# A second-layer feed-forward kernel: split weights kept in DRAM, background work put between a maximum and its split, the last two pairs' operands used in place

## The chip, the cores and the metric

The kernel runs on one core of a Trainium2 chip. The metric is the device time of one execution in microseconds (us). A profile is one further execution, recorded by the hardware profiler; its span runs from its first to its last instruction. Engines are TensorE (PE), VectorE (DVE), ScalarE (ACT), GpSimd (POOL) and SyncE (SP, which here only issues DMAs).

## What is computed

The reference is a gated linear attention (4 batches, 8 heads, 768 steps, head width 48), then a mixture of 8 experts, one for each token, and then a dense feed-forward layer, the "second layer", which is what the change is about:

```python
def _moe2_ref(x, w_in, w_out):      # x: 3072 x 384, w_in: 384 x 2048, w_out: 2048 x 384
    h = x @ w_in
    g = np.maximum(0.01 * h, h)
    return (g @ w_out).astype(np.float32)
```

## The kernel before, in words

All products are float32 in three passes: an operand is split into a rounded high part (`hi`, cast on ScalarE) and a remainder (`lo`, a subtraction on VectorE or GpSimd), and hi·hi, hi·lo and lo·hi are accumulated. That is the helper `split` (L145 the cast, L146 the subtraction).

The program has three stages: the attention (to about 200 us), the experts (to about 381 us) and the second layer, `ffn` (from 381 us to the end). Every engine runs its instructions in the order of the program; SP too issues its DMAs in that order, each after its own waits.

The 3072 tokens of the second layer are cut into six tiles of 512 (`NJ`), the 2048 hidden units into 16 blocks of 128 (`FB`).

**Plain tiles 0 and 1.** The loop counts blocks, n = 0 to 31, 16 for each tile. Block n: nine 512-column products into one of two PSUM banks by turns (L1075); ScalarE makes 0.01·h (`t`, L1079); VectorE takes the maximum of `t` and the bank (L1080), which frees the bank for block n+2; `split` makes `g` of it; the next block's `w_out` rows are split into a tile `wos` (`wosplit`, cast on ScalarE, subtraction on GpSimd); then the second product of block n-2, twelve 384-column products (L1144) into four accumulators (`oacc`); then `more(2)`, two steps of background work. When a tile's last block is done, VectorE and ScalarE copy the accumulators out (L1151); two of the four banks of tile 1's accumulators are banks that tile 0's have used.

**The background** is a generator of steps, mostly on VectorE: first the decoding of the 64-bit weights (L743 to L766, four steps for each half-block), of which 24 steps are left when `ffn` begins; then eight times `forms(m)`: sums and differences of the blocks of pair m's `w_in` (`sums`, L775 to L784) that are split (`forms`: cast L785, subtraction L787) and stored to DRAM (`wfd`). `sums` and `forms` share two buffers (`xw`).

**Tiles 2 to 5** take blocks in pairs, q = 16 to 47, with fewer products: each pair combines its `forms`, loaded back from DRAM into `wf` (L1061), with sums of the tile's columns (`bsum`, `bform`; `bstep` makes those of the next tile). A pair is 33 products of 256 columns (L1088) and 24 of 384 columns (L1144), and splits two blocks' `w_out` rows with `wosplit`. The `wf` of a pair is loaded into one of two `xw` buffers after the last product of the pair two before. The first two, for q = 16 and 17, are loaded at n = 29 and n = 31, after the last `forms`.

Of the kernel before, what the change touches and what calls it, by code (L numbers as in the profile page):

```python
# [83 lines left out]
def kernel(  # L84
# [627 lines left out]
    def experts_and_ffn(place):  # L712
        with ExitStack() as st:
# [5 lines left out]
            wi = [wb.tile([128, 2, 768], FP32R, name=f"wi{i}") for i in range(NM)]  # L719
            wo = [wb.tile([128, 384], FP32, name=f"wo{i}") for i in range(FB)]  # L720
            y = yb.tile([128, 3, NT + GW], FP32, name="y")
# [8 lines left out]
            def decode(i):  # L730
# [34 lines left out]
                if i >= FB:  # L765
                    nc.vector.tensor_tensor(out=wo[i - FB], in0=af, in1=b, op=ALU.add)  # L766
                yield

            def forms(m):

                w = wi[m]
                r = mw.tile([128, 9, 128], FP32, tag="xw", name="sums", bufs=2)
                f = mw.tile([128, 5, 2, 128], FP32R, tag="xw", name="forms", bufs=2)
                tt = nc.vector.tensor_tensor
                tt(out=r[:, 5:9, :].rearrange("p a c -> p (a c)"), in0=w[:, 0, 128:640].bitcast(FP32),  # L775
                   in1=w[:, 1, 128:640].bitcast(FP32), op=ALU.add)
                yield
                a0, b0, a1, b1 = (r[:, 5 + i, :] for i in range(4))
                rr = r[:, 5:9, :].rearrange("p (h i) c -> p h i c", h=2)
                tt(out=r[:, 0:2, :], in0=rr[:, :, 0, :], in1=rr[:, :, 1, :], op=ALU.add)  # L780
                tt(out=r[:, 2, :], in0=a0, in1=b1, op=ALU.add)
# [250 lines left out]
            def bform(j, f):  # L1032
# [3 lines left out]
                else:  # L1036
                    two = ((4, 5), (0, 1), (2, 3), (6, 7), (8, 8))
                    k = [f in x for x in two].index(True)
                    if (j, k) not in bfs:
                        bfs[j, k] = mw.tile([128, 2, 2, HW], FP32R, tag="xT", name="bf", bufs=6)  # L1040
                    t = bfs[j, k][:, two[k].index(f)]
                split(t[:, 0, :], t[:, 1, :], src, nc.vector)
                bfs[j, "f", f] = t

            BSTEPS = {1: ((0, 1), (4,)), 2: ((2, 3), (5,)), 3: ((8,), (0,)), 4: ((), (1, 6)), 5: ((), (2, 7)),
                      6: ((), (3,)), 7: ((), (8,))}

            def bstep(j, m, k):
                for f in BSTEPS.get(m, ((), ()))[k]:
                    (bform if k else bsum)(j, f)  # L1050

            M, NQ = NJ * FB, NJ * NM

            def ffn(key, rest, plain):
                gT, oacc, wos, wf, cap = {}, {}, {}, {}, {}
                tt = nc.vector.tensor_tensor

                def wload2(q):
                    if q < NQ:
                        wf[q] = mw.tile([128, 5, 2, 128], FP32R, tag="xw", name="wf", bufs=2)  # L1060
                        nc.sync.dma_start(out=wf[q].bitcast(FP32), in_=wfd[q % NM])  # L1061

                def wosplit(n):
                    if n < M:
                        w = mw.tile([128, 2, 384], FP32R, tag=f"w{n % 2}", name="wos")
                        split(w[:, 0, :], w[:, 1, :], wo[n % FB], nc.gpsimd)
                        wos[n] = w

                def f1(n):
# [10 lines left out]
                    tt(out=t, in0=t, in1=h_ps, op=ALU.max)  # L1080
                    split(g[:, 0, :], g[:, 1, :], t, nc.vector)
                    gT[n] = [g[:, :, s * 128:(s + 1) * 128] for s in range(4)]

                def mul(q, reg, a, b, first=False):
                    w, x = wi[q % NM], bfs[q // NM, "f", b]
                    c = {5: 128, 6: 512, 7: 0, 8: 640}.get(a)
# [100 lines left out]
                if not plain:  # L1187
                    for m in BSTEPS:
                        for k in range(2):
                            bstep(0, m, k)  # L1190
                    wload2(0)
                    wload2(1)
                for q in range(plain * NM, NQ):
                    j, m = divmod(q, NM)
                    start(q)
                    if q == plain * NM:
                        wosplit(2 * q + 1)
                    wosplit(2 * q + 2)
# [105 lines left out]
```

## Time and profile before

| | |
|---|---|
| median of 3 runs | 795.43 us (795.07 to 795.74) |
| the profiled execution | 797.1 us, of which the span is 795.3 us |
| busy, share of the span | PE 765.3 us (96%), DVE 630.0 (79%), ACT 413.7 (52%), POOL 229.0 (29%) |
| DMA | 112.46 MB, 141 GB/s over the span |
| chain that ended last | PE 70%, DVE 17%, issue 6%, ACT 5%, DMA 1%, POOL 1% |

The profiled execution took 1.7 us more than the median run, and 1.8 us of its time lie outside the span. In a row of the trace the first number is the start in us from the span's start, the second the time from start to end; `x9` are nine instructions merged; `[2.50 <-DVE y L1151]` is idle time of the engine just before, and what ended it. The busy share says little here: TensorE is near its full share in every stage, so the question is in which stretch it stands still.

### The profile page before, as it was taken

Reading aid. Unit: us, or ns where it says so; the run is one execution under the profiler, and the core shown is the slowest. Engines: PE = TensorE matmul, PEld = TensorE weight load, DVE = VectorE, ACT = ScalarE, POOL = GpSimd, SP = SyncE. Lnnn points to the kernel's source line nnn. Section 1 sums busy time; section 2 is a strip of 40 time slices with the busy share of each in tenths; the row PEclk is TensorE's granted clock in tenths of the full one; section 3 lists DMA queues with packets and bytes.
Section 4 is the critical chain, followed back from the end, with each engine's and each line's share of the span. In section 5 each row is a group of like instructions: output and inputs, shape, how many; then the busy total and the mean of one; then the engine's idle time right before and its main releaser. Section 6 shows DMA issues by size and latency. Waiting matters only on the chain.

```text
span 795.3 us, 15530 instructions
## 1 busy us (share of the span) xinstructions
PE 765.3 (96%) x5694; PEld 723.6 (91%) x5695; DVE 630.0 (79%) x1269; ACT 413.7 (52%) x944; POOL 229.0 (29%) x241
## 2 busy tenths in 40 slices
PE   6999998999999999999999999979999999999996
PEld 6888886899999999999889887779999999999996
DVE  8999997668889899989688777768769768766664
ACT  6688775565665656555343344453535444444432
POOL 1322286341111112121222242243233315223221
PEclk9799999999999999999999999999999999999999
DMA  9998834466678678865020021142223233324221
GB/s 347 303 304 281 312 122 130 147 204 212 122 206 212 154 185 216 200 180 140 21 59 21 34 106 66 67 153 90 97 77 129 67 100 106 101 67 132 74 68 44
DMA packets 43221, 112.46 MB, mean 141 GB/s; under 512 B 8256, under 2 KB 19328, under 8 KB 43136
## 3 DMA queue, kind: packets, MB, share of 16 engines
q1 hardware_dynamic: 39296, 101.93, 42.5%
q0 software_dynamic: 3840, 9.47, 3.2%
q8 instruction: 46, 0.75, 0.4%
q14 instruction: 39, 0.32, 0.2%
HBM read 90.36 MB, written 21.01 MB: 140 GB/s over the span
## 4 chain that ended last, share of the span: by engine, by line
PE 70%; DVE 17%; issue 6%; ACT 5%; DMA 1%; POOL 1%; DVEq 0%; POOLq 0%; ACTq 0%; SPq 0%
PE oacc L1144 17%; PE r L1088 15%; PE acc L346 12%; PE h L331 12%; PE A L465 3%; PE X L529 3%; PE Y L519 2%; DVE t L1080 2%; PE Y L513 2%; ACT g L145 2%; DVE g L146 2%; DVE d_t L763 1%; DVE kh L442 1%; DVE sums L775 1%; PE h L1075 1%
## 5 line engine op out<-in xcount | busy, mean ns | idle before, releaser
L1144 PE MATMUL oacc<-wos,g 128*128 128x384 f32 x1152 | 223.1, 338 | 2.5 <-DVE y L1151 2.5
L1144 PEld LDWEIGHTS oacc<-wos,g 128*128 128x128 f32 x1152 | 198.9, 188 | 5.6 <-DVE y L1151 2.8
L146 POOL TENSOR_TENSOR wos<-wo,wos 128x384 fp32r<-128x384 f32 x96 | 100.2, 1059 | 257.8 <-ACT wos L145 254.0
L346 PE MATMUL acc<-hT,w 128*128 128x224 f32 (+7 forms) x648 | 122.5, 333 | 1.4 <-DVE hT L335 1.4
L331 PE MATMUL h<-xT,w 128*128 128x224 f32 (+7 forms) x576 | 114.4, 342 | 0.4 <-DVE w L279 0.4
L346 PEld LDWEIGHTS acc<-hT,w 128*128 128x128 f32 x648 | 109.1, 189 | 4.8 <-DVE hT L335 2.3
L331 PEld LDWEIGHTS h<-xT,w 128*128 128x128 f32 x576 | 98.8, 189 | 3.3 <-DVE w L279 1.0
L273 ACT CAST w<-wraw 128x384 fp32r<-128x384 f32 x138 | 67.5, 513 | 23.4 <-PE acc L346 20.0
L279 DVE TENSOR_TENSOR w<-wraw,w 128x384 fp32r<-128x384 f32 x138 | 72.0, 560 | 6.1 <-ACT w L273 5.2
L1075 PE MATMUL h<-ysp,wi 128*128 128x512 f32 x288 | 72.7, 398 | 3.7 <-DVE t L1080 3.7
L1088 PE MATMUL r<-bf,wi 128*128 128x256 f32 x480 | 68.9, 279 | 0.0
L1075 PEld LDWEIGHTS h<-ysp,wi 128*128 128x128 f32 x288 | 53.1, 188 | 16.1 <-DVE t L1080 5.6
L1123 ACT COPY c<-r 128x256 f32<-128x256 f32 x32 | 11.9, 372 | 107.2 <-PE r L1088 107.2
L1088 PEld LDWEIGHTS r<-bf,wi 128*128 128x128 f32 x480 | 62.6, 188 | 0.0
L334 ACT ACTIVATE hT<-h 128x224 fp32r<-128x224 f32 (+7 forms) x64 | 31.6, 493 | 39.6 <-PE h L331 37.9
L145 ACT CAST g<-t 128x512 fp32r<-128x512 f32 x32 | 19.9, 621 | 62.1 <-DVE t L1080 62.1
L965 POOL COPY seen<-hT 1x1 f32<-1x1 f32 x26 | 7.4, 283 | 150.6 <-DVE hT L335 150.6
L1126 DVE SCALAR_TENSOR_TENSOR c<-c 128x512 f32<-128x512 f32 x64 | 41.4, 688 | 9.8 <-ACT c L1123 8.9
L145 ACT CAST g<-c 128x512 fp32r<-128x512 f32 x64 | 39.2, 622 | 15.4 <-DVE c L1126 14.9
L335 DVE SCALAR_TENSOR_TENSOR hT<-h,hT 128x224 fp32r<-128x224 f32 (+7 forms) x64 | 35.7, 557 | 14.1 <-ACT hT L334 14.1
L449 POOL TENSOR_TENSOR kh<-fkq,kh 128x512 f32<-128x512 f32 x22 | 26.3, 1194 | 70.6 <-DVE kh L442 52.3
L145 ACT CAST wos<-wo 128x384 fp32r<-128x384 f32 x96 | 46.1, 515 | 0.0
(172 smaller groups left out, 1336.7 us busy)
## 6 DMA issues: line engine op xcount, KB each, us to landing
wraw<-in_wpk SPq DMA_DIRECT2D x69, 384.0 KB
wf<-wfd SPq DMA_DIRECT2D x32, 640.0 KB
fkq<-in_fkq SPq DMA_DIRECT2D x21, 770.5 KB
xs<-zero SPq DMA_DIRECT2D x16, 385.0 KB
raw<-in_w_in SPq DMA_DIRECT2D x16, 384.0 KB
raw<-in_w_out SPq DMA_DIRECT2D x16, 384.0 KB
wfd<-forms SPq DMA_DIRECT2D x8, 640.0 KB
v<-in_v SPq DMA_DIRECT2D x24, 192.0 KB
```

The lines of the kernel that those rows point to most:

```text
L145: nc.scalar.copy(out=hi, in_=src)
L146: eng.tensor_tensor(out=lo, in0=src, in1=hi.bitcast(FP32), op=ALU.subtract)
L273: nc.scalar.copy(out=w[:, 0, :], in_=wraw[n][:, 384 * i:384 * (i + 1)])
L279: nc.vector.tensor_tensor(out=w[:, 1, :], in0=r[:, 384 * i:384 * (i + 1)], in1=w[:, 0, :].bitcast(FP32), op=ALU.subtract)
L331: nc.tensor.matmul(out=h_ps, lhsT=w[:, a, kk * 128:(kk + 1) * 128], rhs=xT[p][kk][:, b, :], start=(kk == 0 and a + b == 0), stop=(kk == 2 ...
L334: nc.scalar.activation(out=t[:, 0, :], in_=h_ps, func=ACTF.Relu)
L335: nc.vector.scalar_tensor_tensor(out=t[:, 1, :], in0=h_ps, scalar=0.0, in1=t[:, 0, :].bitcast(FP32), op0=ALU.max, op1=ALU.subtract)
L346: nc.tensor.matmul(out=a_ps[d], lhsT=w[:, a, d * 128:(d + 1) * 128], rhs=t[:, b, :], start=(j == 0 and a + b == 0), stop=(j == KF - 1 and ...
L1075: nc.tensor.matmul(out=h_ps, lhsT=wi[i // 2][:, a, c:c + 128], rhs=ysp[j][kk][:, b, :], start=(kk == 0 and a + b == 0), stop=(kk == 2 and ...
L1088: nc.tensor.matmul(out=reg, lhsT=wf[q][:, a, s, :] if c is None else w[:, s, c:c + 128], rhs=x[:, t, :], start=first and k == 0, stop=k == ...
L1126: nc.vector.scalar_tensor_tensor(out=c, in0=c, scalar=0.01, in1=c, op0=ALU.mult, op1=ALU.max)
L1144: nc.tensor.matmul(out=oacc[j][s], lhsT=gT[n][s][:, b, :], rhs=wos[n][:, a, :], start=i == 0 and a + b == 0, stop=i == FB - 1 and (a, b) = ...
```

## The change

1. `wosplit` splits a block's `w_out` rows only in tile 0, and stores both halves to a DRAM tensor `wod`. From tile 1 on (80 of 96 blocks) it loads them back, three blocks ahead in tile 1 and two pairs ahead later.
2. In the plain tiles one of the two background steps moves in between the maximum and the subtraction of `split` (not at block n = 17). In `bstep` the casts of the next tile's operands stay where they were but for one, and their subtractions move to the next call.
3. `forms` takes its scratch from `wo` (now one tile, dead rows of it) and not from `xw`. The last two `forms`, of pairs 6 and 7, thereby stay in the two `xw` buffers, and q = 16 and 17 use them in place: the order of pairs in a tile becomes 6, 7, 0, ..., 5.

```diff
-            wo = [wb.tile([128, 384], FP32, name=f"wo{i}") for i in range(FB)]
+            wo = wb.tile([128, FB, 384], FP32, name="wo")
...
-                r = mw.tile([128, 9, 128], FP32, tag="xw", name="sums", bufs=2)
-                f = mw.tile([128, 5, 2, 128], FP32R, tag="xw", name="forms", bufs=2)
+                r = wo[:, 0:3, :].rearrange("p a c -> p (a c)").rearrange("p (a c) -> p a c", c=128)
+                f = wfs[m] = mw.tile([128, 5, 2, 128], FP32R, tag="xw", name="forms", bufs=2)
...
-                split(t[:, 0, :], t[:, 1, :], src, nc.vector)
                 bfs[j, "f", f] = t
...
+            def bhi(j, f):
+                src, t = bform(j, f)
+                nc.scalar.copy(out=t[:, 0, :], in_=src)
+                bfs["src"] = bfs.get("src", []) + [(src, t)]
+
+            def blo():
+                for src, t in bfs.pop("src", ()):
+                    nc.vector.tensor_tensor(out=t[:, 1, :], in0=src, in1=t[:, 0, :].bitcast(FP32), op=ALU.subtract)
...
             def bstep(j, m, k):
...
+                for f in BSUMS.get((m, k), ()):
+                    bsum(j, f)
+                blo()
+                for f in BPARTS.get((m, k), ()):
+                    bhi(j, f)
...
+                def pair(q):
+
+                    return (q - 2) % NM
...
-                        nc.sync.dma_start(out=wf[q].bitcast(FP32), in_=wfd[q % NM])
+                        nc.sync.dma_start(out=wf[q].bitcast(FP32), in_=wfd[pair(q)])
...
-                        w = mw.tile([128, 2, 384], FP32R, tag=f"w{n % 2}", name="wos")
-                        split(w[:, 0, :], w[:, 1, :], wo[n % FB], nc.gpsimd)
-                        wos[n] = w
+                        w = wos[n] = mw.tile([128, 2, 384], FP32R, tag=f"w{n % 2}", name="wos")
+                        if n < plain * FB and n < FB:
+                            split(w[:, 0, :], w[:, 1, :], wo[:, n, :], nc.gpsimd)
+                            nc.sync.dma_start(out=wod[n], in_=w.bitcast(FP32))
+                        else:
+                            nc.sync.dma_start(out=w.bitcast(FP32), in_=wod[2 * pair(n // 2) + n % 2 if n >= plain * FB else n % FB])
...
-                    split(g[:, 0, :], g[:, 1, :], t, nc.vector)
+                    nc.scalar.copy(out=g[:, 0, :], in_=t)
+                    if n >= 2 and n != FB + 1:
+                        more(1)
+                    tt(out=g[:, 1, :], in0=t, in1=g[:, 0, :].bitcast(FP32), op=ALU.subtract)
...
-                    wosplit(n + 1)
+                    if n + 1 < FB:
+                        wosplit(n + 1)
+                    if FB <= n + 3 < plain * FB + 2:
+                        wosplit(n + 3)
                     if n >= 2:
                         f2((n - 2,), range(4), of_blocks)
-                        more(2)
+                        more(1)
...
-                    if n >= plain * FB - 3 and i % 2:
-                        wload2(plain * NM + i // 14)
...
+                if plain:
+                    for m in range(2):
+                        wf[plain * NM + m] = wfs[NM - 2 + m]
```

What moves is shown at three places. Line numbers of the kernel after are its own.

VectorE in tile 1, an even and an odd block, before (`t` the maximum, `g` the split's subtraction, `sums` and `forms` the background, `wi` and `bf` subtractions of the next tile's operands):

```order
L1080 TENSOR_TENSOR t<-t,h_6284 128x512
L146 TENSOR_TENSOR g<-t,g 128x512
L775 TENSOR_TENSOR sums<-wi_2557 128x512
L780 TENSOR_TENSOR sums<-sums 128x256
L781 TENSOR_TENSOR sums<-sums 128x128
L1080 TENSOR_TENSOR t<-t,h_6320 128x512
L146 TENSOR_TENSOR g<-t,g 128x512
L783 TENSOR_TENSOR sums<-sums 128x128
L784 TENSOR_TENSOR sums<-sums 128x128
L787 TENSOR_TENSOR forms<-sums,forms 128x5x128
L146 TENSOR_TENSOR wi_2555<-y,wi_2555 128x256
L146 TENSOR_TENSOR bf<-y,bf 128x256
```

and after (`wo` is now the scratch for the sums):

```order
L1102 TENSOR_TENSOR t<-t,h_6272 128x512
L790 TENSOR_TENSOR forms<-wo,forms 128x5x128
L1106 TENSOR_TENSOR g<-t,g 128x512
L778 TENSOR_TENSOR wo<-wi_2558 128x512
L1032 TENSOR_TENSOR y<-y 128x256
L1055 TENSOR_TENSOR wi_2555<-y,wi_2555 128x256
L1102 TENSOR_TENSOR t<-t,h_6308 128x512
L783 TENSOR_TENSOR wo<-wo 128x256
L784 TENSOR_TENSOR wo<-wo 128x128
L1106 TENSOR_TENSOR g<-t,g 128x512
L786 TENSOR_TENSOR wo<-wo 128x128
L787 TENSOR_TENSOR wo<-wo 128x128
```

Each maximum is now followed by one step of background, and only then by the subtraction; the `forms` subtraction has moved past the maximum of the next block.

SP from the end of the experts on, before (`raw` are loads of 64-bit weights for the decoding, `wraw` those of the experts):

```order
L269 DMA wraw<-in_wpk 128x768
L801 DMA idx<-ids 128x24x1
L269 ISA
L269 DMA wraw<-in_wpk 128x768
L728 DMA raw<-in_w_out 128x768 x6
L788 DMA wfd<-forms 128x1280 x8
L1061 DMA wf<-wfd 128x1280 x32
```

and after, to the end of tile 0:

```order
L270 ISA
L270 DMA wraw<-in_wpk 128x768
L729 DMA raw<-in_w_out 128x768
L1087 DMA wod<-wos 128x768 x4
L729 DMA raw<-in_w_out 128x768
L1087 DMA wod<-wos 128x768 x2
L729 DMA raw<-in_w_out 128x768
L1087 DMA wod<-wos 128x768 x2
L729 DMA raw<-in_w_out 128x768
L1087 DMA wod<-wos 128x768 x2
L729 DMA raw<-in_w_out 128x768
L1087 DMA wod<-wos 128x768 x2
```

The loads of `raw` stood in a row with nothing else; now each stands behind two stores of `wod`, which wait for GpSimd.

SP from the last blocks of tile 1 into the pairs, after (before, this was the row of 32 loads of `wf` above):

```order
L791 DMA wfd<-forms 128x1280
L1089 DMA wos<-wod 128x768 x2
L791 DMA wfd<-forms 128x1280
L1089 DMA wos<-wod 128x768 x3
L1080 DMA wf<-wfd 128x1280
L1089 DMA wos<-wod 128x768 x2
L1080 DMA wf<-wfd 128x1280
L1089 DMA wos<-wod 128x768 x2
```

Each pair now has two loads of `wos` and one of `wf`, and there are 30 loads of `wf` where there were 32.

## Rows read from the trace of the kernel before

**Rows 1.** Stretches: busy us (count) by engine, clock, DMA

```profile
core 0: us, PE busy (x) PEld busy (x) DVE busy (x) ACT busy (x) POOL busy (x), PEclk, DMA share, GB/s
...
200.00:368.00 168.00, 168.00 (x932) 163.59 (x931) 149.11 (x333) 100.81 (x218) 30.52 (x47) 1.00 0.74 186
...
516.00:527.00 11.00, 6.54 (x34) 5.74 (x33) 7.52 (x12) 6.10 (x14) 5.44 (x6) 0.93 0.52 179
...
540.00:640.00 100.00, 100.00 (x706) 100.00 (x705) 76.66 (x151) 45.21 (x106) 29.04 (x29) 1.00 0.29 94
```

**Rows 2.** TensorE, blocks n=17 to 19: start, us, form, count, idle

```profile
448.68 2.25 PE L1075 MATMUL h<-ysp,wi 128*128 128x512 f32 x9
...
452.86 2.33 PE L1075 MATMUL h<-ysp,wi 128*128 128x512 f32 x9
455.03 1.21 PE L1144 MATMUL oacc<-wos,g 128*128 128x384 f32 x6
458.74 1.31 PE L1144 MATMUL oacc<-wos,g 128*128 128x384 f32 x6 [2.50 <-DVE y L1151]
459.88 2.25 PE L1075 MATMUL h<-ysp,wi 128*128 128x512 f32 x9
```

**Rows 3.** TensorE, first products of blocks n=24 and n=30

```profile
482.30 2.37 PE L1075 MATMUL h<-ysp,wi 128*128 128x512 f32 x9 [0.73 <-DVE t L1080]
...
511.12 2.36 PE L1075 MATMUL h<-ysp,wi 128*128 128x512 f32 x9 [0.98 <-DVE t L1080]
```

**Rows 4.** Waits from 376 to 516 us: total, times, longest

```profile
DVE g L146 <- ACT g L145: 20.6, 30, 0.7
```

**Rows 5.** VectorE and GpSimd, blocks n=22 and n=23

```profile
482.93 0.69 DVE L146 TENSOR_TENSOR g<-t,g 128x512 fp32r<-128x512 f32 x1 [0.69 <-ACT g L145]
...
483.39 1.11 POOL L146 TENSOR_TENSOR wos<-wo,wos 128x384 fp32r<-128x384 f32 x1 [4.09 <-ACT wos L145]
483.54 1.51 DVE L775 TENSOR_TENSOR sums<-wi 128x512 f32<-128x512 f32 x1
...
490.09 0.82 DVE L787 TENSOR_TENSOR forms<-sums,forms 128x640 fp32r<-128x640 f32 x1 [0.84 <-ACT forms L785]
```

**Rows 6.** The sum of L775 with no GpSimd subtraction beside it

```profile
463.11 0.68 DVE L775 TENSOR_TENSOR sums<-wi 128x512 f32<-128x512 f32 x1
```

**Rows 7.** TensorE at the change to pairs: q=16 (two rows), 17, 18

```profile
520.39 0.62 PE L1088 MATMUL r<-wi,wi 128*128 128x256 f32 x3 [0.65 <-DVE t L1080]
...
524.82 1.82 PE L1088 MATMUL r<-wi,wf 128*128 128x256 f32 x9 [3.81 <-DMA wf<-wfd]
...
534.16 0.51 PE L1088 MATMUL r<-wi,wi 128*128 128x256 f32 x3
...
542.25 0.52 PE L1088 MATMUL r<-wi,wi 128*128 128x256 f32 x3
```

**Rows 8.** Tile 0: a w_out load, a GpSimd subtraction, decode on VectorE

```profile
397.39 9.04 SPq L728 DMA_DIRECT2D raw<-in_w_out  x2
...
399.70 1.11 POOL L146 TENSOR_TENSOR wos<-wo,wos 128x384 fp32r<-128x384 f32 x1 [2.75 <-ACT wos L145]
399.85 1.18 DVE L743 TENSOR_SCALAR d_t<-raw 128x384 int32<-128x384 int32 x1
...
408.56 1.18 DVE L743 TENSOR_SCALAR d_t<-raw 128x384 int32<-128x384 int32 x1
```

**Rows 9.** DMA, 396 to 406 us in 40 slices: GB/s

```profile
GB/s 0 0 0 0 0 0 0 0 0 147 184 135 197 406 406 98 0 0 0 0 0 0 0 0 0 0 0 0 0 0 0 0 0 0 0 0 0 0 0 0
```

**Rows 10.** DMA, 518 to 528 us in 40 slices: GB/s, then the total

```profile
GB/s 0 0 0 0 0 0 0 0 0 492 451 369 430 369 328 184 164 266 266 328 328 451 410 307 266 102 123 307 348 389 348 430 266 143 0 0 0 0 0 0
DMA packets 432, 1.97 MB, mean 197 GB/s; under 512 B 48, under 2 KB 48, under 8 KB 432
```

**Rows 11.** A wf issue; GB/s from 561 to 571 us, 40 slices

```profile
563.55 8.40 SPq L1061 DMA_DIRECT2D wf<-wfd  x2
...
GB/s 0 0 0 0 0 0 0 0 0 0 0 0 0 20 184 143 184 389 348 389 430 328 123 82 0 0 0 0 0 0 0 66 0 0 0 0 0 0 0 0
```

More of the change, by code (lines that the diff above doesn't have):

```diff
@@ L135 @@
     wfd = dram.tile([NM, 128, 5, 2, 128], FP32, name="wfd")
+    wod = dram.tile([FB, 128, 2, 384], FP32, name="wod")
     def scatter_rows(key, dst, at, src, limit):
@@ L765, in decode @@
                 if i >= FB:
-                    nc.vector.tensor_tensor(out=wo[i - FB], in0=af, in1=b, op=ALU.add)
+                    nc.vector.tensor_tensor(out=wo[:, i - FB, :], in0=af, in1=b, op=ALU.add)
                 yield
+            wfs = {}
             def forms(m):
                 w = wi[m]
-                r = mw.tile([128, 9, 128], FP32, tag="xw", name="sums", bufs=2)
-                f = mw.tile([128, 5, 2, 128], FP32R, tag="xw", name="forms", bufs=2)
+                r = wo[:, 0:3, :].rearrange("p a c -> p (a c)").rearrange("p (a c) -> p a c", c=128)
+                f = wfs[m] = mw.tile([128, 5, 2, 128], FP32R, tag="xw", name="forms", bufs=2)
                 tt = nc.vector.tensor_tensor
@@ L1041, in bform @@
                     t = bfs[j, k][:, two[k].index(f)]
-                split(t[:, 0, :], t[:, 1, :], src, nc.vector)
                 bfs[j, "f", f] = t
-            BSTEPS = {1: ((0, 1), (4,)), 2: ((2, 3), (5,)), 3: ((8,), (0,)), 4: ((), (1, 6)), 5: ((), (2, 7)),
-                      6: ((), (3,)), 7: ((), (8,))}
-            def bstep(j, m, k):
-                for f in BSTEPS.get(m, ((), ()))[k]:
-                    (bform if k else bsum)(j, f)
+                return src, t
+            def bhi(j, f):
[5 more added lines that the diff above has]
+                    nc.vector.tensor_tensor(out=t[:, 1, :], in0=src, in1=t[:, 0, :].bitcast(FP32), op=ALU.subtract)
+            BSUMS = {(1, 0): (0, 1), (2, 0): (2,), (3, 0): (3,), (4, 0): (8,)}
+            BPARTS = {(1, 1): (4,), (2, 1): (5,), (3, 1): (0,), (4, 1): (1, 6), (5, 1): (2, 7), (6, 1): (3,), (7, 0): (8,)}
+            def bstep(j, m, k):
+                for f in BSUMS.get((m, k), ()):
[3 more added lines that the diff above has]
+                    bhi(j, f)
             M, NQ = NJ * FB, NJ * NM
@@ L1080, in f1 @@
                     tt(out=t, in0=t, in1=h_ps, op=ALU.max)
-                    split(g[:, 0, :], g[:, 1, :], t, nc.vector)
+                    nc.scalar.copy(out=g[:, 0, :], in_=t)
+                    if n >= 2 and n != FB + 1:
+                        more(1)
+                    tt(out=g[:, 1, :], in0=t, in1=g[:, 0, :].bitcast(FP32), op=ALU.subtract)
                     gT[n] = [g[:, :, s * 128:(s + 1) * 128] for s in range(4)]
                 def mul(q, reg, a, b, first=False):
-                    w, x = wi[q % NM], bfs[q // NM, "f", b]
+                    w, x = wi[pair(q)], bfs[q // NM, "f", b]
                     c = {5: 128, 6: 512, 7: 0, 8: 640}.get(a)
@@ L1184, in ffn @@
                         nc.gpsimd.drain()
-                    if n >= plain * FB - 3 and i % 2:
-                        wload2(plain * NM + i // 14)
-                if not plain:
-                    for m in BSTEPS:
+                if plain:
+                    for m in range(2):
+                        wf[plain * NM + m] = wfs[NM - 2 + m]
+                else:
+                    wosplit(1)
+                    for m in range(NM):
                         for k in range(2):
@@ L1195, in ffn @@
                     start(q)
-                    if q == plain * NM:
-                        wosplit(2 * q + 1)
                     wosplit(2 * q + 2)
```

## The prediction, made before the kernel after was run

> **What bounds the kernel now.** I read the page's busy shares first, then stretches of the span, then TensorE in time at the places where a stretch shows it idle, and last what those idle times waited for. The experts (200 to 368 us) and the pairs (540 to 640 us) leave TensorE no idle time at all [rows 1]. A pair takes 100 us / (706 / 57 products) = 8.07 us there, and 542.25 - 534.16 = 8.09 us between the starts of the second and third pair [rows 7]. In the plain tiles a block takes 452.86 - 448.68 = 4.18 us when TensorE waits for nothing [rows 2]. So work that is taken from ScalarE, GpSimd or VectorE counts for nothing by itself. What can be won is the time in which TensorE stands still between block n = 18 and the second pair (q = 17), and after q = 17 nothing.
>
> That window: block 18 starts at 452.86 us, q = 17 at 534.16 [rows 2, 7]. Without a wait it would hold 14 blocks and one pair, 14 x 4.18 + 8.08 = 66.6 us. It holds 81.3 us. The difference is 14.7 us, in three pieces:
> - A, block 18: from its start to the next is 459.88 - 452.86 = 7.02 us, 2.84 more than 4.18. TensorE waits 2.50 us for the copy that empties an accumulator bank of tile 0 (`y`, L1151) [rows 2]: VectorE is more than a block late, and the copy stands behind the work of earlier blocks.
> - B, blocks 19 to 31: 13 x 4.18 = 54.3 us from 459.88 end at 514.22; q = 16 starts at 520.39 [rows 7], 6.17 us late. From n = 24 to n = 30, six blocks take 511.12 - 482.30 = 28.82 us, 9.61 for two where 8.36 would do, and the idle time ends with VectorE's maximum (`t`, L1080) [rows 3], which frees the bank. VectorE bounds this stretch.
> - C, pair q = 16: 534.16 - 520.39 = 13.77 us, 5.69 more than 8.08. TensorE waits 3.81 us for the first load of `wf` [rows 7]; the rest is in step with a granted clock of 0.93 in that stretch, so part of it at the lower of TensorE's two levels (1.2 instead of 2.4 GHz), after the idle time [rows 1].
>
> **The change, part by part.**
>
> *Last two pairs in place.* q = 16 and 17 need no load: `forms` for pairs 6 and 7 are finished on VectorE at n = 28 and n = 30, before q = 16 by more than a block. The 3.81 us go, and with no idle time ahead there is no reason for the low clock. C: -5.69 us. What is late next is the load for q = 18, which cannot be issued before the last product of q = 16 has read its buffer. It then has the rest of that pair (twelve second products, some 2 us) and all of q = 17, some 10 us. Alone, such a load goes from issue at 563.55 to its last bytes at 567.0, 3.45 us [rows 11]; three transfers of that size in flight together took 520.25 to 526.5, 6.25 us [rows 10]. Both are under 10 us: cost 0. The other end is that C's wait comes back there (rival 2).
>
> *Background between maximum and subtraction.* VectorE waits for the cast of `g` 0.69 us in 30 blocks, 20.6 us in all [rows 4], and in an odd block another 0.84 us for the cast of `forms` [rows 5]. Both get work in front of them now: the step in between is 0.7 us or more in every block of tile 1 but n = 17 and the last, and `forms`' subtraction has moved past a maximum. From 9.61 us for two blocks go 2 x 0.69 + 0.84 = 2.22: 7.39 us, less than TensorE's 8.36. B goes (-6.17 us), unless a new wait stands in the way (rival 1).
>
> A is the lateness that VectorE gathers in tile 0. There it needs 408.56 - 399.85 = 8.71 us for two blocks [rows 8], 0.35 more than TensorE, and three blocks also split an operand of tile 1, about 0.7 us each like the subtraction of `g`: over some six twos 6 x 0.35 + 3 x 0.7 = 4.2 us. So the bank that could be copied from 452.86 on, when block 18 starts, comes free at 458.74 [rows 2]. Now one block of two has a decode step to put in, the other an empty one, so one wait of 0.69 goes: 8.02 us, and 6 x (8.02 - 8.36) + 2.1 leaves next to nothing. The first six products of block 16's second half need other banks (455.03 and 1.05 us on), so the copy has until 456.1, some 2 us to spare. A goes: -2.84 us.
>
> GpSimd's subtraction costs VectorE time as well. The sum of L775 takes 1.51 us with such a subtraction beside it (it starts 0.15 us later) [rows 5], and 0.68 us without [rows 6]. In the words of the Trainium skill (SBUF — State Buffer, "Who interferes with whom"), a VectorE instruction with two SBUF inputs and a GpSimd instruction that reads SBUF shut each other out, and the later one waits for the whole of the other; this trace agrees, 0.83 us in that row. By that rule tile 1, now without those subtractions, would need 7.39 - 2 x 0.83 = 5.7 us for two blocks. Neither figure reaches 8.36, so it is no term of the sum; it makes rival 1 less likely.
>
> *Split weights in DRAM.* 80 casts and 80 GpSimd subtractions go, off the path. Added are 16 stores and 80 loads of 384 KB on SP, 37.7 MB. In tile 1 and in the pairs the loads are asked for three blocks and two pairs ahead, 12 to 16 us, against 2.6 us for one of 384 KB (issue 397.39 [rows 8], last bytes at 400.0 [rows 9]). In tile 0 each load of `raw` now stands behind a store that waits for GpSimd. The issue moves from 397.39 to the end of the split at 399.70 + 1.11 = 400.81 [rows 8], and two transfers of 2.6 us end by 406.0. What was issued at 397.39 is first used at 408.56 [rows 8], or half a microsecond sooner now: 2 us to spare, cost 0; a late load would hold up VectorE, not TensorE at once. In the pairs DMA rises by 2 x 0.393 MB / 8.08 us = 97 GB/s to about 191 GB/s. The nearest row is the experts' stretch, 186 GB/s at a share of 0.74, with TensorE busy all through [rows 1]: cost 0. The other end is rival 3.
>
> **The sum.** 2.84 + 6.17 + 5.69 = 14.7 us. The profiled execution would take 797.1 - 14.7 = 782.4 us with a span of 780.6. The median of the runs is 1.67 us under that execution, so 795.43 - 14.7 = **780.7 us**. A gain beyond that needs a block under 4.18 us or a pair under 8.07 us, for which no row gives a reason, or a shorter tail; I leave 1.7 us below for the differences of runs and reading.
>
> **Rivals.**
>
> *1. VectorE and ScalarE stay the bound in tile 1.* ScalarE works in order: the copy `t` of the next block stands behind the cast of `forms` and those of the next tile's operands, and these now wait for sums that VectorE does later in its block. If two blocks take 9.0 us and not 8.36, the six twos after n = 19 cost 3.8 us: 784.5 us. If A and B stay as they are, 780.7 + 9.0 = 789.7 us. For it: the empty steps and n = 17 keep their wait, and the slack in tile 0 is only 8.36 - 8.02 = 0.34 us. Against: 7.39 us without counting what GpSimd gives back. 14 in 100, the smaller price the likelier.
>
> *2. The wait moves to q = 18*, the first pair whose `wf` is loaded: at most C again, 786.4 us. For it: the load has two loads of `wos` behind and ahead of it. Against: 10 us for 3.45 to 6.25. 7 in 100.
>
> *3. The queue becomes the bound of the pairs*, and the kernel is slower. If the three loads of a pair pass one after the other, they take 2 x 2.6 + 3.45 = 8.65 us, 0.57 more than a pair. After the lead of two pairs, 30 pairs x 0.57 = 17 us are lost: 797.8 us. It decides for slower from 8.08 + 14.7 / 30 = 8.57 us on. Against it: three transfers of 640 KB did not pass one after the other but took 6.25 us together [rows 10], 315 GB/s, by which a pair's 1.44 MB take 4.6 us. 5 in 100.
>
> The Trainium skill (DMA: Bandwidth & Descriptors, from its fixed cost of about 2.0 us for each DMA and 436 GB/s, and its rule to batch to 1 MiB) speaks for rival 3: an estimate by that page, if nothing overlapped, is 2 x 2.9 + 3.5 = 9.3 us for a pair and some 817 us in all. The trace's 6.25 us for three says that they overlap.
>
> *4. Nothing is won*, because a new wait between stores and loads of `wod` or the shared scratch takes the place of all three: 795 us. 2 in 100.
>
> **How the numbers follow.** The forecast has 72 in 100 (779.0 to 782.5 by itself), the rivals 14, 7, 5 and 2. The range 779.0 to 787.0 us holds the forecast, rival 2 and over half of rival 1, some 87 in 100. This kernel's runs differ by 0.1%, so that about 0.2% can be told from no change: faster 0.93, same 0.02, slower 0.05.
>
> **What would show it.** Right: q = 16's first product at about 511.4 us and q = 17's at 519.5; no idle TensorE from n = 18 on; blocks 4.18 us apart to n = 31; pairs still 8.07 us; clock 1.00 in the first pair; GpSimd busy about 229 - 80 x 1.1 = 141 us; 112.5 + 37.7 - 1.3 = 148.9 MB moved. Wrong: maxima (`t`) that still end TensorE's idle time (rival 1), a wait for `wf` at q = 18 (rival 2), or pairs longer than 8.1 us with a wait for `wos` or `wf` (rival 3).

## The result, and the profile after

The kernel after takes 781.1 us (median of 4 runs, 780.46 to 781.59), the kernel before 795.59 in the same comparison: a ratio of 0.982 (0.980 to 0.983), 14.5 us less. Forecast were 780.7 us, 14.7 less.

The profiled execution after has a span of 779.7 us. Of its page, first the busy times, then all that DMA moved:

```profile
PE 760.0 (97%) x5694; PEld 722.1 (93%) x5695; DVE 606.7 (78%) x1269; ACT 383.4 (49%) x864; POOL 147.5 (19%) x161
...
DMA packets 56759, 148.93 MB, mean 191 GB/s; under 512 B 9760, under 2 KB 20832, under 8 KB 56672
```

GpSimd is busy for 147.5 us where 141 were expected: its splits of `wos` took 100.2 us before and the 16 that are left take 19.3, so the 80 that went were a little shorter than the 1.1 us that the forecast gave them. The bytes are the 148.9 MB of the forecast. TensorE in time, block 18 and the first three pairs (start, us, form, count, and in brackets idle time, of which there is none):

```profile
451.49 2.25 PE L1097 MATMUL h<-ysp,wi 128*128 128x512 f32 x9
453.58 2.25 PE L1169 MATMUL oacc<-wos,g 128*128 128x384 f32 x12
455.67 2.27 PE L1097 MATMUL h<-ysp,wi 128*128 128x512 f32 x9
...
510.11 0.52 PE L1113 MATMUL r<-wi,wi 128*128 128x256 f32 x3
510.46 1.23 PE L1113 MATMUL r<-wi,forms 128*128 128x256 f32 x9
...
518.19 0.51 PE L1113 MATMUL r<-wi,wi 128*128 128x256 f32 x3
...
526.27 0.52 PE L1113 MATMUL r<-wi,wi 128*128 128x256 f32 x3
526.63 1.23 PE L1113 MATMUL r<-wi,wf 128*128 128x256 f32 x9
```

Read this against [rows 2, 3, 7]. Block 18 takes 455.67 - 451.49 = 4.18 us, where it took 7.02. The pair q = 16 takes 518.19 - 510.11 = 8.08 us, where it took 13.77, and q = 18, the first that loads its `wf`, starts those products with no wait. From block 18 to q = 17 it is 518.19 - 451.49 = 66.70 us, where it was 81.30: 14.60 us are gone. The rest of the difference of the spans (15.6 us) is a second layer that starts 1.35 us sooner, which varies from one profiled execution to the next (block 0 started between 380.3 and 383.0 us in all the traces here), and a tail from q = 17 that is 261.51 us, 0.37 longer. Two stretches of the trace after (columns as in [rows 1]):

```profile
512.00:527.00 15.00, 15.00 (x108) 15.00 (x107) 10.75 (x23) 5.45 (x13) 3.87 (x4) 1.00 0.61 211
540.00:640.00 100.00, 100.00 (x707) 100.00 (x706) 71.27 (x149) 35.24 (x82) 3.87 (x4) 1.00 0.56 189
```

The clock in the first pairs is 1.00, and the pairs do 707 products in 100 us as before, with twice the DMA. VectorE in two blocks of tile 1 after, with one row of ScalarE, and VectorE's last subtraction for `forms`:

```profile
479.59 0.69 DVE L1102 TENSOR_TENSOR t<-t,h 128x512 f32<-128x512 f32 x1 [1.70 <-ACT t L1101]
480.19 0.82 DVE L790 TENSOR_TENSOR forms<-wo,forms 128x640 fp32r<-128x640 f32 x1
480.96 0.69 DVE L1106 TENSOR_TENSOR g<-t,g 128x512 fp32r<-128x512 f32 x1
481.57 0.68 DVE L778 TENSOR_TENSOR wo<-wi 128x512 f32<-128x512 f32 x1
...
483.15 0.60 ACT L1101 ACTIVATE t<-h 128x512 f32<-128x512 f32 x1 [2.22 <-PE h L1097]
483.78 0.69 DVE L1102 TENSOR_TENSOR t<-t,h 128x512 f32<-128x512 f32 x1 [0.86 <-ACT t L1101]
...
505.31 0.82 DVE L790 TENSOR_TENSOR forms<-wo,forms 128x640 fp32r<-128x640 f32 x1
```

The `forms` subtraction and `g` no longer wait ([rows 5] had 0.84 and 0.69 us), the sum of L778 takes 0.68 us and not 1.51, and VectorE now waits for ScalarE's `t` (1.70 and 0.86 us). In the block of 0.86 us ScalarE in turn waits 2.22 us for TensorE's products; in the other `t` stands behind ScalarE's casts of `forms` and of the next tile's operand. TensorE has no idle time in either, so VectorE is ahead of it.

So the number and the three pieces came out as forecast. What that doesn't tell is which part of the change did it.

### The profile page after: what moved, and what is told of

It is laid out like the page before. It is cut to its first block, busy times and chain, and to the rows that moved or that the text cites. A ratio compares the mean times of both kernels' runs of the same rounds, so it can differ in the third digit from the quotient of the medians.

```text
span 779.7 us, 15515 instructions
## 1 busy us (share of the span) xinstructions
PE 760.0 (97%) x5694; PEld 722.1 (93%) x5695; DVE 606.7 (78%) x1269; ACT 383.4 (49%) x864; POOL 147.5 (19%) x161
## 4 chain that ended last, share of the span: by engine, by line
issue 42%; PE 41%; DVE 11%; POOL 2%; ACT 2%; POOLq 1%; another core or an unknown queue 0%; DMA 0%; DVEq 0%; ACTq 0%
PE acc L347 13%; PE h L332 12%; PE X L530 3%; PE A L466 2%; PE h L1097 2%; PE Y L520 2%; POOL out L139 2%; PE Y L514 2%; PE oacc L1169 2%; DVE w L280 1%; DVE kh L443 1%; PE xt L317 1%; DVE qh L457 1%; DVE am L473 1%; PE KV L493 1%
## 5 line engine op out<-in xcount | busy, mean ns | idle before, releaser
L139 POOL DMA_INDIRECT out<-y,idx x24 | 23.9, 994 | 310.8 <-DVE y L1176 303.5
L147 DVE TENSOR_TENSOR g<-c,g 128x512 fp32r<-128x512 f32 x64 | 41.6, 689 | 3.2 <-ACT g L146 0.4
L1102 DVE TENSOR_TENSOR t<-t,h 128x512 f32<-128x512 f32 x32 | 21.9, 686 | 25.1 <-ACT t L1101 25.1
L1147 DVE TENSOR_TENSOR c<-t,r 128x256 f32<-128x256 f32 x32 | 13.5, 421 | 35.2 <-PE r L1113 35.1
L1101 ACT ACTIVATE t<-h 128x512 f32<-128x512 f32 x32 | 19.1, 597 | 42.6 <-PE h L1097 42.5
```

Source lines behind the costliest of these rows:

```text
L139: ins = nc.gpsimd.indirect_dma_start(out=dst, out_offset=bass.IndirectOffsetOnAxis(ap=at, axis=0), in_=src, in_offset=None, bounds_check=l ...
```

## Experiments

The parts are D (split weights kept in DRAM), B (background between maximum and subtraction) and P (last two pairs in place). The diffs show the lines that matter; names, buffers, places of calls and the order of pairs, which follow from them, are left out. e12 is the changed kernel run once more. The kernel before was run again beside each group of experiments, and its median differs (795.59 us above, 798.38 beside e1 to e4, 797.01 beside e5 to e8, 796.71 beside e9 to e12). Block 0's start moves too, so each kernel is also read from its trace by the time that TensorE lost in the pieces of the prediction: A (block 18), B (blocks 19 to 31), C (q = 16), each by the same start-to-start sums. A trace is one execution: the runs of e2 lie between 789.18 and 793.24 us, those of e4 between 783.86 and 786.87 (its trace is of the slowest), so the losses of these two differ between executions.

| kernel | parts | us | ratio to before | A | B | C | lost in all |
|---|---|---|---|---|---|---|---|
| before | none | | 1 | 2.84 | 6.17 | 5.69 | 14.70 |
| e1 | P | 794.88 | 0.995 (0.993 to 0.997) | 3.79 | 4.89 | 3.59 | 12.27 |
| e2 | B | 791.99 | 0.992 (0.989 to 0.995) | 0.02 | 1.16 | 8.27 | 9.45 |
| e3 | D | 785.56 | 0.984 (0.982 to 0.986) | 1.21 | 0.08 | 0.39 | 1.68 |
| e4 | D, B | 786.38 | 0.984 (0.982 to 0.986) | 0.00 | 0.10 | 3.95 | 4.05 |
| e5 | B, P | 787.94 | 0.988 (0.986 to 0.991) | 0.00 | 0.82 | 3.93 | 4.75 |
| e6 | D, P | 783.57 | 0.983 (0.980 to 0.985) | 1.20 | 0.08 | 0.00 | 1.28 |
| after | D, B, P | 781.10 | 0.982 (0.980 to 0.983) | 0.00 | 0.10 | 0.00 | 0.10 |
| e7 | D, casts given back | 783.96 | 0.983 (0.981 to 0.986) | 1.18 | 0.08 | 0.00 | 1.26 |
| e8 | D, subtractions given back | 798.94 | 1.002 (1.001 to 1.003) | 3.03 | 6.58 | 6.99 | 16.60 |

### One part alone

**e1: in place alone.** Without D the rows of `wo` are still wanted, so the scratch of the sums lies in two `raw` buffers. Against before:

```diff
-                r = mw.tile([128, 9, 128], FP32, tag="xw", name="sums", bufs=2)
+                ra = dec.tile([128, 768], I32, tag="raw", name="raw", bufs=2)[:, 0:512].bitcast(FP32).rearrange("p (a c) -> p a c", c=128)
+                r = dec.tile([128, 768], I32, tag="raw", name="raw", bufs=2)[:, 0:640].bitcast(FP32).rearrange("p (a c) -> p a c", c=128)
...
-                    if n >= plain * FB - 3 and i % 2:
-                        wload2(plain * NM + i // 14)
...
+                if plain:
+                    for m in range(2):
+                        wf[plain * NM + m] = wfs[NM - 2 + m]
```

> The last two pairs' operands in place and nothing else of the change (the scratch of the sums lies in two buffers that the decoding has done with; every block is still split on ScalarE and GpSimd). Theory: A (2.84 us) and B (6.17) are VectorE's lateness and stay, only C (5.69) goes: 795.4 - 5.7 = 789.7 us, with blocks of tile 1 still 4.8 us apart and no wait for wf at the first pair. Rival, that the late wf was what held everything (more buffers for forms also free VectorE): about 781.

It won 2.43 us of the 14.70, and of C, which it should have taken away, 2.10 of 5.69. A grew by 0.95 us; why isn't shown. TensorE at q = 16 in e1:

```profile
520.18 0.62 PE L1099 MATMUL r<-wi,wi 128*128 128x256 f32 x3 [0.55 <-DVE t L1091]
522.46 1.67 PE L1099 MATMUL r<-wi,forms 128*128 128x256 f32 x9 [1.66 <-DVE t L1091]
```

The wait for the load has become a wait for a maximum on VectorE. C was not a load's lateness alone: behind the load stood VectorE's.

**e2: background alone.** The hunks on `f1`, `bhi`, `blo` and `bstep`; the last `forms` end later by it, so the loads of `wf` go to n = 30 and 31. Against before:

```diff
-                    split(g[:, 0, :], g[:, 1, :], t, nc.vector)
+                    nc.scalar.copy(out=g[:, 0, :], in_=t)
+                    if n >= 2 and n != FB + 1:
+                        more(1)
+                    tt(out=g[:, 1, :], in0=t, in1=g[:, 0, :].bitcast(FP32), op=ALU.subtract)
...
-                        more(2)
+                        more(1)
...
-                    if n >= plain * FB - 3 and i % 2:
-                        wload2(plain * NM + i // 14)
+                    if n >= plain * FB - 2:
+                        wload2(plain * NM + i - 14)
```

> Only the background between maximum and subtraction, and the late subtractions of the next tile's operands; no DRAM copies, nothing in place (the first two wf are loaded at blocks 30 and 31, since the last forms end at 30). Theory: two blocks need 7.4 us on VectorE even with GpSimd's subtractions beside it, so A and B go (9.0 us): 786.4 us if C stays as it was. C should shrink too, because the forms end early against TensorE and the load has some 4 us more: down to 781.5. Rival, GpSimd's port is what makes VectorE late: A and B stay in good part, 790 or more.

A goes in full, B to 1.16 us, and C, which was to shrink, grows to 8.27. TensorE at q = 16 in e2:

```profile
514.26 0.50 PE L1109 MATMUL r<-wi,wi 128*128 128x256 f32 x2 [2.13 <-DVE wi L1055]
517.85 2.26 PE L1109 MATMUL r<-wi,wf 128*128 128x256 f32 x9 [3.09 <-DMA wf<-wfd]
```

The operand of the next tile (`wi`) and the last `forms` are late on VectorE, and the load with them. Part of what B wins is put off to the first pair.

**e3: DRAM copies alone.** The hunks on `wosplit` and its calls. Against before:

```diff
-                        split(w[:, 0, :], w[:, 1, :], wo[n % FB], nc.gpsimd)
+                        if n < plain * FB and n < FB:
+                            split(w[:, 0, :], w[:, 1, :], wo[:, n, :], nc.gpsimd)
+                            nc.sync.dma_start(out=wod[n], in_=w.bitcast(FP32))
+                        else:
+                            nc.sync.dma_start(out=w.bitcast(FP32), in_=wod[2 * pair(n // 2) + n % 2 if n >= plain * FB else n % FB])
...
-                    wosplit(n + 1)
+                    if n + 1 < FB:
+                        wosplit(n + 1)
+                    if FB <= n + 3 < plain * FB + 2:
+                        wosplit(n + 3)
```

> Only the split weights in DRAM: no GpSimd subtractions from tile 1 on, everything else as before. Theory with the port counted: two blocks of tile 1 need 9.61 - 1.67 = 7.9 us on VectorE, under TensorE's 8.36, so B goes and with it most of C; A stays, since tile 0 still splits: 783.5 to 786 us. Theory without the port: VectorE's waits for ScalarE stay, A, B and C stay: 795 us. Rival, the DMAs of the pairs cost: above 796, with pairs longer than 8.1 us.

This part, which the prediction had costed at nothing, wins 13.02 of the 14.70 us by itself; A, which was to stay, falls to 1.21. What is left of A, and q = 16, in e3:

```profile
458.39 1.31 PE L1158 MATMUL oacc<-wos,g 128*128 128x384 f32 x6 [0.94 <-DVE y L1165]
...
513.96 0.52 PE L1102 MATMUL r<-wi,wi 128*128 128x256 f32 x3
514.64 1.30 PE L1102 MATMUL r<-wi,wf 128*128 128x256 f32 x9 [0.17 <-DMA wf<-wfd]
```

The load of `wf`, at its old place in the program, costs 0.17 us of waiting. Why it cost 3.81 us before is told by VectorE's last `forms` subtraction, after which the buffer for the load comes free, first in before and then in e3 (with the issue of the load):

```profile
518.58 0.83 DVE L787 TENSOR_TENSOR forms<-sums,forms 128x640 fp32r<-128x640 f32 x1 [0.84 <-ACT forms L785]
```

```profile
507.77 0.83 DVE L790 TENSOR_TENSOR forms<-sums,forms 128x640 fp32r<-128x640 f32 x1 [0.84 <-ACT forms L788]
...
508.99 0.42 SPq L1072 DMA_DIRECT2D wf<-wfd  x1
```

Before, it ends 1.0 us ahead of q = 16 (520.39 - 519.41), in e3 5.4 us (513.96 - 508.60). With VectorE on time, the load is issued on time.

### One part undone

**e4: not in place** (D and B). Against after, with `pair(q)` as `q % NM` and the scratch in `xw` again:

```diff
-                if plain:
-                    for m in range(2):
-                        wf[plain * NM + m] = wfs[NM - 2 + m]
-                else:
+                    if n >= plain * FB - 2:
+                        wload2(plain * NM + i - 14)
+                if not plain:
```

> The changed kernel without the last two pairs in place (their forms are stored and loaded at blocks 30 and 31, in the old order of pairs): DRAM copies and background moved stay. Theory: A and B gone (9.0 us), 786.4 us if C stays whole; since forms end some 4.7 us before the first pair and a load takes 3.5 to 6.3 us, a wait of 0 to 2 us is left of C: 781 to 783.5 us. Rival, C is a piece of its own that only the in-place operands remove: 786.4.

It loses 3.95 us in C, where e3 lost 0.39 and a wait of 0 to 2 was expected. The last `forms` subtraction, the issue of the loads, the first row of q = 16 that waits and one row after it, in e4:

```profile
506.61 0.82 DVE L790 TENSOR_TENSOR forms<-sums,forms 128x640 fp32r<-128x640 f32 x1
...
508.34 2.94 SPq L1080 DMA_DIRECT2D wf<-wfd  x2
...
514.15 1.31 PE L1113 MATMUL r<-wi,wf 128*128 128x256 f32 x9 [2.18 <-DMA wf<-wfd]
...
516.96 0.84 PE L1113 MATMUL r<-wi,wf 128*128 128x256 f32 x3
```

That subtraction ends 4.0 us before q = 16 starts (511.46 - 507.43), where e3 had 5.4: the moved background ends the `forms` later, and the buffers come free later with them. The load is issued 3.12 us ahead of q = 16 (511.46 - 508.34), in e3 4.97 (513.96 - 508.99): of the 1.85 us of difference 1.3 are the `forms`, and the rest is that in e4 a load of `wos` stands ahead of it on SP. Of the 3.95 us the wait is 2.18; most of the rest is in step with the granted clock, 0.86 over this pair in e4 and 1.00 in e3's, with three products at 0.84 us instead of 0.52. Using the buffers in place is what pays for all that; it belongs to B, as a repair, more than it is a gain of its own.

**e5: no DRAM copies** (B and P, scratch as in e1). Against after:

```diff
-                        if n < plain * FB and n < FB:
-                            split(w[:, 0, :], w[:, 1, :], wo[:, n, :], nc.gpsimd)
-                            nc.sync.dma_start(out=wod[n], in_=w.bitcast(FP32))
-                        else:
-                            nc.sync.dma_start(out=w.bitcast(FP32), in_=wod[2 * pair(n // 2) + n % 2 if n >= plain * FB else n % FB])
+                        split(w[:, 0, :], w[:, 1, :], wo[:, 2 * pair(n // 2) + n % 2 if n >= plain * FB else n % FB, :], nc.gpsimd)
```

> The changed kernel without the DRAM copies (every block still split on ScalarE and GpSimd): background moved and last two pairs in place. The prediction's own reading, that these two parts carry the whole gain: A and C at 0, B at 1 us or less, about 14 us gained. The reading after the runs of single parts, that GpSimd's subtractions still make VectorE late at the end of tile 1: B 1.2 us as with the background alone, and 1.5 to 4 us of C left as a wait for VectorE at the first pair; 9.5 to 12 us gained.

It loses 4.75 us. This is the run that tests the prediction's 7.39 us for two blocks. ScalarE, GpSimd and VectorE in e5, blocks 28 to 31, and TensorE at q = 16 (only the rows named below; the sums are written to `raw` here):

```profile
495.62 1.10 POOL L147 TENSOR_TENSOR wos<-wo,wos 128x384 fp32r<-128x384 f32 x1 [4.09 <-ACT wos L146]
495.77 1.50 DVE L779 TENSOR_TENSOR raw<-wi 128x512 f32<-128x512 f32 x1
...
497.86 0.68 DVE L1099 TENSOR_TENSOR t<-t,h 128x512 f32<-128x512 f32 x1
...
501.17 0.73 ACT L789 CAST forms<-raw 128x640 fp32r<-128x640 f32 x1 [1.56 <-DVE raw L788]
...
502.11 0.40 ACT L1051 CAST bf<-y 128x256 fp32r<-128x256 f32 x1
502.42 0.59 ACT L1098 ACTIVATE t<-h 128x512 f32<-128x512 f32 x1
503.04 0.69 DVE L1099 TENSOR_TENSOR t<-t,h 128x512 f32<-128x512 f32 x1 [1.90 <-ACT t L1098]
...
507.13 0.68 DVE L1099 TENSOR_TENSOR t<-t,h 128x512 f32<-128x512 f32 x1
...
512.01 0.69 DVE L1099 TENSOR_TENSOR t<-t,h 128x512 f32<-128x512 f32 x1 [1.60 <-ACT t L1098]
...
515.26 0.80 PE L1110 MATMUL r<-wi,wi 128*128 128x256 f32 x2 [2.13 <-DVE wi L1056]
```

From one maximum to that two blocks on it is 507.13 - 497.86 = 9.27 us, and 512.01 - 503.04 = 8.97 us for the other pair of them. The waits for `g` and `forms` are gone but for 0.15 us, and a new one stands in the odd block: ScalarE casts `forms` only when VectorE's sums are done (501.17), then the next tile's operands, then makes `t`; VectorE waits 1.90 us for it. 7.39 + 1.90 = 9.29 us and, for the other, 7.39 + 1.60 = 8.99, within 0.02 us of what was measured. (e5 gives ScalarE's casts of `wos` back as well as GpSimd's subtractions. These casts aren't on this path: ScalarE stands idle for 1.56 us before the cast of `forms`.) That is rival 1, at its price of 9.0 us for two blocks or a little above. TensorE shows only 0.82 us of it in blocks 19 to 31, where rival 1 had 3.8: it keeps its pace to block 29 (499.47 - 453.41 = 46.06 us for 11 blocks) and is late only after that, so VectorE, on time at block 18 (A is 0.00), falls behind for a dozen blocks before TensorE has to wait. The rest comes due at q = 16, where `wi` is late (2.13 us).

**e6: background not moved** (D and P; the hunks on `bhi`, `blo` and `bstep` are undone too). Against after:

```diff
-                    nc.scalar.copy(out=g[:, 0, :], in_=t)
-                    if n >= 2 and n != FB + 1:
-                        more(1)
-                    tt(out=g[:, 1, :], in0=t, in1=g[:, 0, :].bitcast(FP32), op=ALU.subtract)
+                    split(g[:, 0, :], g[:, 1, :], t, nc.vector)
...
-                        more(1)
+                        more(2)
```

> The changed kernel with the background steps and subtractions where they were: DRAM copies and last two pairs in place stay. Theory (VectorE is freed in tile 1 by the DRAM copies, and the moved background counts in tile 0 alone): A 1.2 us as with the copies alone, B and C 0: 13.5 us gained of 14.7. Rival, that the moved background is needed in tile 1 too: B above 2 us, under 12 us gained.

1.20 us are lost, all in A. VectorE's 30 waits for `g` ([rows 4]: 20.6 us) are all still there in e6:

```profile
DVE g L147 <- ACT g L146: 20.6, 30, 0.7
```

Yet B is 0.08 us. Of the two shares of VectorE's time, waits of 2.22 us and GpSimd's 1.66 us for two blocks, taking away the second alone is enough: 9.61 - 1.66 = 7.95, under TensorE's 8.36. e7 below, which has the same waits for `g`, measures it where VectorE still catches up: 498.99 - 491.08 = 7.91 us for two blocks.

### What in the DRAM copies it is: e7 and e8

D takes a cast from ScalarE and a subtraction from GpSimd in every block. e7 and e8 are e3 with one of them given back in blocks 15 to 31; what they make is used by nothing. e7 and e8 against e3:

```diff
+                    if FB - 1 <= n < plain * FB:
+                        nc.scalar.copy(out=wo[:, 0, :].bitcast(FP32R), in_=wo[:, n % FB, :])
```

```diff
+                    if FB - 1 <= n < plain * FB:
+                        nc.gpsimd.tensor_tensor(out=wo[:, 0, :], in0=wo[:, n % FB, :],
+                                                in1=ghi[n][:, 0:384].bitcast(FP32), op=ALU.subtract)
```

> DRAM copies alone, with one cast of 128x384 on ScalarE put back into each of blocks 15 to 31, whose result nothing uses. If the copies help because ScalarE, which works in order, has 0.5 us less in each block ahead of the next block's copy: A and B come back, some 5 to 8 us lost against the copies alone. If they help through GpSimd: 0 to 0.5 us lost, blocks of tile 1 stay at 4.18 us.

> DRAM copies alone, with one subtraction of 128x384 on GpSimd put back into each of blocks 15 to 31, whose result nothing uses; it starts when the block's high part is there. If VectorE is late because GpSimd's subtractions hold up its instructions (0.83 us each): A 2.8 and B 3 to 6 us come back, some 5 to 9 us lost against the copies alone. If ScalarE's casts were the cause: 0 to 0.5 us lost.

The casts cost nothing (1.26 us lost, in e3 1.68). The 17 subtractions cost 798.94 - 783.96 = 15.0 us against e7: all that D had won, and 2 us more. ScalarE and VectorE in e7 (the row of L1191 is the cast given back, the first and the last row are maxima two blocks apart):

```profile
491.08 0.68 DVE L1094 TENSOR_TENSOR t<-t,h 128x512 f32<-128x512 f32 x1
...
492.32 0.51 ACT L1191 CAST wo<-wo 128x384 fp32r<-128x384 f32 x1
...
493.05 0.68 DVE L778 TENSOR_TENSOR sums<-wi 128x512 f32<-128x512 f32 x1
...
498.99 0.68 DVE L1094 TENSOR_TENSOR t<-t,h 128x512 f32<-128x512 f32 x1
```

and VectorE, GpSimd (the subtraction given back) and TensorE in e8:

```profile
482.60 0.69 DVE L147 TENSOR_TENSOR g<-t,g 128x512 fp32r<-128x512 f32 x1 [0.74 <-ACT g L146]
482.71 1.46 POOL L1191 TENSOR_TENSOR wo<-wo,g 128x384 f32<-128x384 f32 x1 [3.80 <-ACT g L146]
483.20 1.50 DVE L778 TENSOR_TENSOR sums<-wi 128x512 f32<-128x512 f32 x1
...
487.65 1.11 DVE L786 TENSOR_TENSOR sums<-sums 128x128 f32<-128x128 f32 x1
488.68 0.28 DVE L787 TENSOR_TENSOR sums<-sums 128x128 f32<-128x128 f32 x1
...
491.61 2.37 PE L1089 MATMUL h<-ysp,wi 128*128 128x512 f32 x9 [0.81 <-DVE t L1094]
...
525.21 2.26 PE L1103 MATMUL r<-wi,wf 128*128 128x256 f32 x9 [4.19 <-DMA wf<-wfd]
```

The sum takes 1.50 us beside the subtraction, 0.68 in e7; in the next block the 128x128 sum takes 1.11 us where the one after it takes 0.28. The trace of e8 loses 16.60 - 1.68 = 14.9 us more than e3's, with the waits of before: for `y` in A (3.03), for maxima in B (6.58), for `wf` in C (6.99). Expected were 5 to 9 us, from A and B; C, which comes back whole, wasn't counted. The blocked time itself, some 0.82 us in each of 17 blocks, is 14 us of VectorE's, but that it is near 14.9 is chance: 0.4 of the 1.66 us for two blocks is slack against TensorE (8.36 - 7.95), and C holds a load's way and a granted clock of 0.77 over the pair besides.

### The queue and the rest

**e9, e10: more loads in the pairs.** The changed kernel with two and with four further loads of 384 KB for each pair, into rows of `wo` that nothing reads any more. e10 (e9 has 2 for 4):

```diff
+                    for x in range(4):
+                        at = 2 * ((4 * q + x) % 8)
+                        nc.sync.dma_start(out=wo[:, at:at + 2, :], in_=wod[(2 * q + x) % FB])
```

> The changed kernel with two more loads of 384 KB from DRAM in every pair, into dead rows of wo, used by nothing: 2.23 MB for each pair, 275 GB/s. Theory, the queue has room (three transfers of 640 KB took 6.25 us together, 315 GB/s) and DMA does not slow TensorE: pairs stay at 8.08 us, 0 to 0.3 us lost. Rival 3 of the prediction, transfers pass one after the other at 2.6 and 3.45 us: 13.9 us for a pair, far above 900 us in all.

> The same with four more loads in every pair: 3.0 MB for each, 373 GB/s at 8.08 us. At the 315 GB/s that the trace of the kernel before showed for three transfers, a pair needs 9.5 us and some 40 us are lost, with waits for wos or wf in every pair. At the highest slices of that trace (over 400 GB/s) a pair needs 7.4 us and nothing is lost.

781.97 us (ratio 0.981, 0.979 to 0.984) and 782.06 (0.981, 0.979 to 0.983), against 782.21 for e12. Two stretches of e10 (columns as above), then its loads in 8.08 us, the length of a pair (KB each, us from issue to landing; the third `wos` belongs to a neighbouring pair):

```profile
540.00:640.00 100.00, 100.00 (x707) 100.00 (x706) 70.61 (x148) 34.88 (x81) 3.88 (x4) 1.00 1.01 383
640.00:740.00 100.00, 100.00 (x709) 100.00 (x708) 68.54 (x142) 32.89 (x75) 7.75 (x8) 1.00 1.01 389
```

```profile
wo<-wod SPq DMA_DIRECT2D x4, 384.0 KB, 7.3
wos<-wod SPq DMA_DIRECT2D x3, 384.0 KB, 5.9
wf<-wfd SPq DMA_DIRECT2D x1, 640.0 KB, 6.7
```

The DMA engines are busy all the time (share 1.01) with twice the bytes of after, and TensorE still does 707 products in 100 us. The 383 to 389 GB/s are above the 315 that three transfers had in [rows 10]. Rival 3 is far off: one after the other, the seven loads of a pair in e10 would take 6 x 2.6 + 3.45 = 19.05 us, and they pass in 8.08.

**e11: the step at block 17 too.**

```diff
-                    if n >= 2 and n != FB + 1:
+                    if n >= 2:
```

> The changed kernel with the background step also put between maximum and subtraction at block 17, which the change leaves out. Theory: VectorE is not late by then and the copy out of tile 0's accumulators has about 2 us to spare, so the step of about 0.5 us costs nothing: A 0 to 0.2 us. Rival, the exemption is what takes A away: 0.5 us or more of A comes back.

781.67 us (0.981, 0.979 to 0.983); A is 0.02 us. The exemption of block 17 is not needed.

**e12: the changed kernel again.**

> The changed kernel itself once more, for its time on the chip of the three others: 14 to 15 us under the kernel before.

782.21 us (0.982, 0.979 to 0.984), 0.08 us lost. No kernel here beats the changed one by more than its runs differ, and no idle time is left in the window that a further one could take.

## Why the number was right, and where the reasons were not

- **The sum** of 14.7 us was made of TensorE's idle time against a block of 4.18 and a pair of 8.08 us. That needs no knowledge of causes, only that all of the idle time goes, and it held: 14.60 us. After q = 17 nothing was won, as forecast. That all of it went was in part luck: with B and P alone, which the prediction had carry the whole, 4.75 us stay (e5, a gain of 9.1 us). The part that was costed at nothing brought the rest.
- **"It is no term of the sum"** (GpSimd's 0.83 us) **and "off the path"** (80 subtractions) is the step that failed. It is the largest term: D alone wins 13.02 of 14.70 us, e8 against e7 shows that it is the subtractions, and e8's rows show how: without them two blocks take VectorE 7.91 us and not 9.61 (e7 against before), and TensorE's 8.36 lies between. The prediction had read the row that shows it (L775, 1.51 us) but compared only the end of its reckoning, 7.39 or 5.7 us, with TensorE's 8.36. In the words of the Trainium skill (SBUF — State Buffer, "Who interferes with whom"), a VectorE instruction with two inputs in SBUF and a GpSimd instruction that reads SBUF shut each other out. e8 agrees: 0.68 us become 1.50. The prediction had this rule and its row, and used them only for a chance.
- **9.61 - 2.22 = 7.39 us for two blocks** failed for the background alone. e5 has 9.27 and 8.97, since the wait for `t` (1.90 us) takes the place of those that were removed. Rival 1 had named that mechanism with nearly its price, but gave it 14 in 100 as a case of the whole change. With D it doesn't bite: after has the same wait for `t`, but there VectorE waits ahead of TensorE.
- **A** was right in its mechanism: B alone removes it (e2, 0.02 us left). But D alone also takes it from 2.84 to 1.21 us. It is lateness, and time given to VectorE by either part pays it.
- **C, "the 3.81 us go"** by using operands in place: right for the whole, but not for P. P alone leaves 3.59 of 5.69 us, and D alone, with the load as before, 0.39. The load was late because `forms` were, 1.0 us ahead of q = 16 before. The prediction asked only when they are done in the kernel after, "by more than a block" ahead; there it is 510.11 - 506.13 = 3.98 us, a little less than a block. With VectorE on time by D, P takes away what is left; without D a wait for VectorE stands in the load's place (e1, e5).
- **The parts don't add.** Alone they win 2.43, 5.25 and 13.02 us in the traces, 20.7 together, where there are 14.7 to win. All three pieces hung on one cause, VectorE's lateness. Once D is there, B is worth 1.2 us (e6), and P 0.4 (e3 against e6) or, with B, 3.9 (e4). Without P, B then costs 2.4 us in the traces (e3 against e4); the times of these two, 785.56 and 786.38 us, can't be told apart.
- **The queue** and the wait at q = 18 were right: no wait, 189 GB/s in the pairs for about 191, and room for twice that (e10).

What stays open is tile 0, where GpSimd still subtracts beside VectorE in the kernel after; that wasn't tried, since TensorE has no idle time there to win.

## What to carry to other kernels

Idle time of the bound engine, summed against its undisturbed pace, was here a good forecast of the most that could be won; which edit wins it is a second question, and where one late engine lies behind several stalls their shares don't add over the edits. When one row shows an instruction stretched by a neighbour, count the stretch on the late engine's side and compare its total with the bound engine's pace, with and without it: 9.61 and 7.95 us against 8.36 told the outcome here. And before a wait is counted as removed, follow the engine that it waited for to its next instruction: in e5 ScalarE, working in order, handed the wait on (1.90 us for the 2.22 that were removed).

## What the runs showed of the hardware

- A GpSimd subtraction that starts 0.11 us after a VectorE one with two inputs in SBUF takes 1.46 us (1.11 in [rows 5], where it starts 0.46 us after one), and VectorE's next is held up by 0.82 us (1.50 for 0.68) or 0.83 (1.11 for 0.28): the same loss for an instruction of 512 columns and for one of 128.
- One queue of transfers of 384 and 640 KB kept up 383 to 389 GB/s for 200 us while TensorE had no idle time and the times of VectorE and ScalarE didn't grow (70.6 and 34.9 us busy in 100, after 71.3 and 35.2). The Trainium skill (SBUF — State Buffer, "Who interferes with whom") states that DMA never contends with a compute engine, and this trace agrees for these three engines at a full share (1.01). The fixed cost of about 2.0 us for each DMA that the Trainium skill gives (DMA: Bandwidth & Descriptors) doesn't add up here: the loads of a pair overlap, seven in 8.08 us, and land 5.9 to 7.3 us after their issue.
